# A group normalisation rewritten with hand-set semaphores: PE and VectorE in loops, VectorE taking over GpSimd's scaling and part of PE's sums

## Chip, cores, metric

One core of a Trainium2 chip. The metric is the device time of one launch in microseconds (us). Both kernels were timed several times; nearly all runs of a kernel agree within 0.3%. The record marks every run as fast or slow, by its time against the fastest run of the same kernel; all runs quoted here were fast, except that a single run (e4, e7) has no such mark.

Names: PE is the matrix engine, DVE is VectorE, ACT is ScalarE, POOL is GpSimd, SP is the engine that issues the transfers. A "DMA engine" is one of the core's 16 transfer engines. PSUM is the memory that PE writes its sums to; a chunk is 512 neighbouring elements of a partition's row.

## The reference

```python
# x: (128, 1024, 32, 16) bf16; g, b: (1024,) bf16; G = 32 groups of 32 channels
xr = x.reshape(B, G, C // G, H, W)
mu = xr.mean(axis=(2, 3, 4), keepdims=True)
var = ((xr - mu) ** 2).mean(axis=(2, 3, 4), keepdims=True)
xn = ((xr - mu) / jnp.sqrt(var + 1e-5)).reshape(B, C, H, W)
return xn * g[None, :, None, None] + b[None, :, None, None]
```

The input is 134 MB and the output is 134 MB. A tile is 4 samples by 32 groups on 128 partitions, with 32 channels of 512 elements along a partition: 4 MB (4096 KB in the profile). There are 32 tiles, numbered 0 to 31.

## The kernel before

It is written in a framework that sets the waits by itself. Six slots hold tiles. Cut to what the argument touches:

```python
XBUFS = 6; UPFRONT = 6; AHEAD = 5; QUARTERS = 4
STORE_IN_PARTS = 2; LAST_SHARE = 3; POOL_SHARE = 13
...
def L(i):                                  # load, on SP's queue
    xt = xpool.tile([P, F], BF16, name="xt")
    parts = NQ if i == 0 or i >= NT - 1 else 1
    w = F // parts
    for c in range(parts):
        ... nc.sync.dma_start(out=xt[:, c*w:(c+1)*w], in_=x_v[i][:, c*w:(c+1)*w])
...
def matmuls(st, name, lo, hi):             # PE adds the 32 chunks of a tile in PSUM
    for k in range(lo, hi):
        ... matmul(out=ps, lhsT=eye, rhs=st["xt"][:, k*MMN:(k+1)*MMN], ...)
...
def squares(st, w, k, bias, scale, sq):    # ACT, two halves per tile, sum in accum_out
...
def A(i):                                  # scale and shift: POOL 13 channels, DVE 16
    if not in_parts(i):
        for n in range(POOL_SHARE):
            scale_on("pool", i, KC - LAST_SHARE - POOL_SHARE + n)
        for k in range(KC - LAST_SHARE - POOL_SHARE):
            scale_on("dve", i, k)
    ...                                    # last two tiles: stores in quarters
def finish(i):                             # ACT takes the last 3 channels
    for k in range(KC - LAST_SHARE, KC):
        scale_on("act", i, k)
    S(i, 0, NQ)                            # one store of the tile
    j = i + AHEAD
    if UPFRONT <= j < NT:
        L(j)                               # waits until the store of tile i-1 has landed
...
for i in range(NT):
    Q(i)                                   # squares of i, with finish(i-1) in the middle
    if i + 1 < NT:
        M(i + 1); R0(i + 1)                # sums of i+1
    V(i)                                   # 1/sqrt, then scale and shift factors
    A(i)
```

## Time and profile before

| | before |
|---|---|
| time, median | 634.59 us when it was given; 634.62 us in four runs beside the changed kernel |
| profiled span | 631.9 us |
| bytes moved | 268.44 MB |
| rate, 61 to 552 us | 432 GB/s, DMA share 1.00 |
| busy ACT / DVE / POOL / PE | 85% / 60% / 55% / 46% |
| spacing of the stores in the middle | 19.4 us |

From the profile's page: the busy time of each engine; then the DMA share and the rate in 40 equal slices of the span (9 means at least 90%); then the data queue with packets, MB and share of 16 engines' span.

```profile
span 631.9 us, 3907 instructions
...
PE 293.1 (46%) x1025; PEld 114.4 (18%) x1025; DVE 380.2 (60%) x645; ACT 539.0 (85%) x268; POOL 346.8 (55%) x523
...
DMA  8999999999999999999999999999999999999996
GB/s 365 431 437 423 430 431 429 431 433 431 424 430 432 431 431 429 430 433 438 428 432 429 433 431 429 430 430 433 434 431 431 430 430 432 433 426 436 433 418 271
...
q1 hardware_dynamic: 10944, 268.44, 99.0%
```

No compute engine is above 85%, the queue is at 99%. The first slice is a ramp and the last slice a tail; between them the rate stays near 431.

The groups of instructions: count, then busy us and mean ns of one, then the idle time before them and what ended it.

```profile
L244 ACT ACTIVATE ja<-xt,negmean 128x8192 fp8e5<-128x8192 bf16 x60 | 426.7, 7112 | 52.1 <-DVE jd L189 52.0
...
L368 DVE TENSOR_SCALAR xt<-xt,scl,bia 128x512 bf16<-128x512 bf16 x536 | 352.6, 732 | 40.0 <-POOL bia L353 40.0
L368 POOL TENSOR_SCALAR xt<-xt,scl,bia 128x512 bf16<-128x512 bf16 x390 | 308.7, 806 | 3.4 <-POOL bia L353 0.3
```

ScalarE has 60 such squares of 7.1 us; the scaling of a channel is recorded as 732 ns on DVE and 806 ns on POOL.

Busy time in four stretches, from the table of windows (start and end in us, length, busy us and counts by engine, PE clock, DMA share, GB/s; other windows below have the same columns, less the engines that were idle throughout):

```profile
core 0: us, PE busy (x) PEld busy (x) DVE busy (x) ACT busy (x) POOL busy (x), PEclk, DMA share, GB/s
61.00:552.00 491.00, 231.47 (x800) 89.70 (x800) 312.24 (x499) 440.55 (x211) 299.52 (x446) 0.71 1.00 432
600.00:616.00 16.00, 0.00 (x0) 0.00 (x0) 11.04 (x37) 10.95 (x13) 0.00 (x0) 0.50 0.98 415
616.00:624.00 8.00, 0.00 (x0) 0.00 (x0) 0.00 (x0) 0.00 (x0) 0.00 (x0) 0.50 1.00 421
624.00:632.00 8.00, 0.00 (x0) 0.00 (x0) 0.00 (x0) 0.00 (x0) 0.00 (x0) 0.50 0.29 123
```

Steady transfers hold to 624 us. All arithmetic has ended by 616 us, and the last 8 us are DMA engines finishing at different times: the 16 completions of the last store come between 623.81 and 630.98 us.

SP's issues from the timeline, which show the steady rhythm (start us, us, engine, line, operation, out<-in, count; the same columns in every timeline below):

```profile
start us, us, engine line op out<-in xcount [idle before <-releaser]
...
435.47 0.34 SPq L101 DMA_DIRECT2D xt<-in_x_dram  x1
435.91 0.37 SPq L381 DMA_DIRECT2D out_dram<-xt  x1
454.84 0.34 SPq L101 DMA_DIRECT2D xt<-in_x_dram  x1
```

Each load is issued when the store that last used its slot has landed, and the next store follows at once; a pair comes every 19.4 us, which is 8.39 MB (one load and one store of 4.19 MB) at 432 GB/s. The store was ready and queued behind the waiting load.

DVE's scaling of tiles 29 and 30 from the timeline:

```profile
574.25 11.14 DVE L368 TENSOR_SCALAR xt<-xt,scl,bia 128x512 bf16<-128x512 bf16 x16 [1.29 <-POOL bia L353]
...
591.23 5.26 DVE L368 TENSOR_SCALAR xt<-xt,scl,bia 128x512 bf16<-128x512 bf16 x16 [1.29 <-POOL bia L353]
```

Sixteen channels take 11.14 us while POOL scales too, and 5.26 us when POOL rests, a factor of 2.1.

### The profile page before, as it was taken

How to read it: one execution, taken by the hardware profiler on the slowest of the kernel's cores; microseconds unless marked ns; L12 is line 12 of the kernel's file. 1: busy time of each engine (PE TensorE's matmuls, PEld its weight loads, DVE VectorE, ACT ScalarE, POOL GpSimd, SP SyncE). 2: the span in 40 equal slices, each digit the busy share in tenths (PEclk: the TensorE clock that was granted, in tenths of full speed). 3: DMA queues.
4: the chain of work that ended last, by engine and by line, in shares of the span. 5: the costliest groups of instructions: out<-in, count | busy, mean ns of one | idle time of the engine just before them, and what ended most of it. 6: DMA issues, size and time to landing. Idle time of an engine off the chain costs nothing.

```text
span 631.9 us, 3907 instructions
## 1 busy us (share of the span) xinstructions
PE 293.1 (46%) x1025; PEld 114.4 (18%) x1025; DVE 380.2 (60%) x645; ACT 539.0 (85%) x268; POOL 346.8 (55%) x523
## 2 busy tenths in 40 slices
PE   5578604553245633456433565335553345647000
PEld 2233201221112211122111222112221112213000
DVE  1087666666676576545775457754657654577660
ACT  4589999999999897877997779977989797797960
POOL 0077666666666576544775446764557654477100
PEclk9689758766787657876678766677865788658655
DMA  8999999999999999999999999999999999999996
GB/s 365 431 437 423 430 431 429 431 433 431 424 430 432 431 431 429 430 433 438 428 432 429 433 431 429 430 430 433 434 431 431 430 430 432 433 426 436 433 418 271
DMA packets 11063, 268.70 MB, mean 425 GB/s; under 512 B 1312, under 2 KB 1312, under 8 KB 1312
## 3 DMA queue, kind: packets, MB, share of 16 engines
q1 hardware_dynamic: 10944, 268.44, 99.0%
q8 instruction: 8, 0.13, 0.1%
q14 instruction: 15, 0.12, 0.0%
q10 hardware_dynamic: 96, 0.00, 0.0%
HBM read 134.22 MB, written 134.22 MB: 425 GB/s over the span
## 4 chain that ended last, share of the span: by engine, by line
DMA 67%; ACT 15%; PE 7%; issue 4%; DVE 3%; POOL 0%; SPq 0%; DVEq 0%; ACTq 0%; POOLq 0%
DMA out_dram<-xt 42%; DMA xt<-in_x_dram 25%; ACT ja L244 13%; PE pa L166 7%; DVE xt L368 3%; ACT xt L363 2%; DMA gb_b<-in_g_dram 1%; POOL scl L337 0%; SPq L101 0%; ACT rstd L308 0%; DVE rstd L312 0%; DVE jd L189 0%; POOL shift L343 0%; DVEq L455 0%; DVE bia L324 0%
## 5 line engine op out<-in xcount | busy, mean ns | idle before, releaser
L244 ACT ACTIVATE ja<-xt,negmean 128x8192 fp8e5<-128x8192 bf16 x60 | 426.7, 7112 | 52.1 <-DVE jd L189 52.0
L166 PE MATMUL pa<-xt,eye 128*128 128x512 bf16 x976 | 281.8, 460 | 289.7 <-DMA xt<-in_x_dram 278.5
L368 DVE TENSOR_SCALAR xt<-xt,scl,bia 128x512 bf16<-128x512 bf16 x536 | 352.6, 732 | 40.0 <-POOL bia L353 40.0
L368 POOL TENSOR_SCALAR xt<-xt,scl,bia 128x512 bf16<-128x512 bf16 x390 | 308.7, 806 | 3.4 <-POOL bia L353 0.3
L166 PEld LDWEIGHTS <-eye 128*128 128x128 bf16 x1024 | 114.3, 114 | 468.5 <-DMA xt<-in_x_dram 290.6
L337 POOL TENSOR_SCALAR scl<-gb,rstd 128x32 f32<-128x32 f32 x31 | 11.2, 361 | 218.2 <-DVE rstd L312 218.2
L189 DVE TENSOR_SCALAR_CACHE_REDUCE jd<-pa 128x512 bf16<-128x512 f32 x32 | 22.0, 688 | 149.0 <-PE pa L166 149.0
L363 ACT ACTIVATE xt<-xt,bia,scl 128x512 bf16<-128x512 bf16 x98 | 72.0, 798 | 0.8 <-DVE bia L324 0.8
L244 ACT ACTIVATE ja<-xt,q 128x4096 fp8e5<-128x4096 bf16 x8 | 29.6, 3706 | 6.6 <-DVE jd L189 6.4
L312 DVE RECIPROCAL rstd<-rstd 128x1 f32<-128x1 f32 x32 | 5.1, 160 | 35.8 <-ACT rstd L308 35.8
L343 POOL TENSOR_SCALAR shift<-scl,negmean 128x32 f32<-128x32 f32 x31 | 11.2, 360 | 3.1
L216 POOL TENSOR_SCALAR off<-negmean,q 128x1 f32<-128x1 f32 x2 | 0.9, 432 | 20.5 <-DVE jd L189 20.5
L166 PE MATMUL pb<-xt,eye 128*128 128x512 bf16 x48 | 11.6, 388 | 1.0 <-DMA xt<-in_x_dram 1.0
L308 ACT ACTIVATE rstd<-s,v 128x1 f32<-128x1 f32 x30 | 8.8, 294 | 2.8
L244 ACT ACTIVATION_READ_ACCUMULATOR ja<-xt,negmean 128x1 f32 x60 | 11.2, 187 | 0.0
L353 POOL TENSOR_TENSOR bia<-shift,gb 128x32 f32<-128x32 f32 x31 | 7.8, 252 | 2.6
L308 ACT ACTIVATE rstd<-var,eps_t 128x1 f32<-128x1 f32 x2 | 0.6, 295 | 9.2 <-DVE jv L292 9.2
L273 POOL TENSOR_SCALAR v<-s 128x1 f32<-128x1 f32 x30 | 5.8, 192 | 2.5
L156 DVE COPY gb<-gb_p 128x64 f32<-128x64 f32 x1 | 0.2, 224 | 5.6 <-PE gb_p L148 5.6
L116 ACT ACT_TABLE_LOAD x1 | 1.3, 1283 | 1.7 <-PEq L444 1.7
L189 DVE DVE_READ_ACCUMULATOR jd<-pa 128x1 f32 x32 | 2.6, 81 | 0.0
L292 DVE TENSOR_SCALAR_CACHE_REDUCE jv<-sq,seed 128x4 f32<-128x4 f32 x2 | 0.4, 216 | 2.7 <-ACT ja L244 2.7
(18 smaller groups left out, 6.1 us busy)
## 6 DMA issues: line engine op xcount, KB each, us to landing
xt<-in_x_dram SPq DMA_DIRECT2D x30, 4096.0 KB, 29.3
out_dram<-xt SPq DMA_DIRECT2D x30, 4096.0 KB, 38.3
xt<-in_x_dram SPq DMA_DIRECT2D x8, 1024.0 KB, 16.5
out_dram<-xt SPq DMA_DIRECT2D x8, 1024.0 KB, 17.8
gb_b<-in_g_dram ACTq DMA_DIRECT2D x1, 2.0 KB, 3.2
gb_b<-in_b_dram ACTq DMA_DIRECT2D x1, 2.0 KB, 5.3
```

The source lines that it names most:

```text
L116: chain("act", nc.scalar.activation(out=warm[:], in_=eps_t[:], func=ACT.Sqrt))
L166: nc.tensor.matmul(out=ps[:], lhsT=eye[:], rhs=st["xt"][:, k * MMN : (k + 1) * MMN], start=(k == lo), stop=(k == hi - 1),),
L189: nc.vector.tensor_scalar(out=jd[:], in0=ps[:], scalar1=-inv_n, scalar2=seed, op0=ALU.mult, op1=ALU.add, accum_out=total[:],),
L244: nc.scalar.activation(out=ja[:, 0:w], in_=st["xt"][:, k * w : (k + 1) * w], func=ACT.Square, bias=bias, scale=scale, accum_out=sq, satura ...
L273: nc.gpsimd.tensor_scalar(out=v0[:], in0=s0[:], scalar1=inv_n, scalar2=EPS, op0=ALU.mult, op1=ALU.add,),
L308: nc.scalar.activation(out=rstd[:], in_=last_sum[:], func=ACT.Sqrt, bias=bias[:], scale=scale),
L312: chain("dve", nc.vector.reciprocal(out=rstd[:], in_=rstd[:]))
L337: nc.gpsimd.tensor_scalar(out=scl[:], in0=gam, scalar1=rstd[:], scalar2=None, op0=ALU.mult),
L343: nc.gpsimd.tensor_scalar(out=shift[:], in0=scl[:], scalar1=st["negmean"][:], scalar2=None, op0=ALU.mult,),
L353: nc.gpsimd.tensor_tensor(out=bia[:], in0=shift[:], in1=bet, op=ALU.add),
L363: inst = nc.scalar.activation(out=span, in_=span, func=ACT.Identity, bias=bia, scale=scl)
L368: inst = eng.tensor_scalar(out=span, in0=span, scalar1=scl, scalar2=bia, op0=ALU.mult, op1=ALU.add,)
```

## The change

The intent: take the framework's waits and the sharing between DVE and POOL out of the way, and balance the work. Each engine gets its own program; PE and DVE loop over six tiles a trip. POOL scales nothing, DVE scales 29 channels; PE adds 20 chunks and DVE the other 12, as pairs. The scale and shift factors move from POOL to DVE, which summed the means before too. The core of the diff:

```diff
-XBUFS = 6
-UPFRONT = 6
+SLOTS = 6
+FIRST = 2
 AHEAD = 5
-STORE_IN_PARTS = 2
-ACT_SHARE = 2
-LAST_SHARE = 3
-POOL_SHARE = 13
+PE_CHUNKS = 20
+ACT_SHARE = 3
+LAST_ACT_SHARE = 4
...
+    loaded = per_slot("loaded")        # 14 semaphores for each of 6 slots, and 5 more
+    stored = per_slot("stored")
...
+    ctx.callback(lambda: nc.clear_and_free_semaphores(sems))
+    block = ctx.enter_context(nc.Block())
+    @block.sync
+    def _(sp):
...
+        for i in range(SLOTS):
+            load(i)                    # each in one piece
+        for i in range(NT):
+            n = nth(i)
+            if i < NT - 1:
+                store(i, 0, KC, n, n)
+            else:
+                store(i, 0, KC // 2, n, n)
+                store(i, KC // 2, KC, n + 1, n + 1)
+            j = i + AHEAD
+            if SLOTS <= j < NT:
+                load(j)
...
+    @block.tensor
+        with loop(pe):                 # 20 matmuls a tile, six tiles a trip
+            for i in range(FIRST, FIRST + SLOTS):
+                add_chunks(*in_loop(i, regs["w1"], regs["w2"]))
...
+    @block.vector
+        def mean(s, count, count16):
+            inst = dve.scalar_tensor_tensor(   # 3072 pairs, the other 12 chunks
+                out=jd[:],
+                in0=xts[s][:, PE_CHUNKS * MMN : PE_CHUNKS * MMN + PAIRS],
+                scalar=1.0,
+                in1=xts[s][:, PE_CHUNKS * MMN + PAIRS : F],
+                op0=ALU.mult, op1=ALU.add, accum_out=col(s, HALF), ...
+        with loop(dve):
+            for i in range(FIRST, FIRST + SLOTS):
+                ...
+                mean(s, c, w)
+                ...
+                factors(s, c)
+                apply(s, 0, KC - ACT_SHARE, c)
...
+    @block.scalar                      # ACT: as before, but no early root, and all tiles in halves
+        for i in range(NT):
+            squares(i, 0)
+            if i:
+                apply(i - 1, KC - ACT_SHARE, KC)
+            squares(i, 1)
+            root(i)
```

## The prediction

> **What bounds the kernel now.** The transfers. The page shows 268.44 MB on the one data queue, busy for 99.0% of 16 engines' span, mean 425 GB/s. The table of windows gives 432 GB/s from 61 to 552 us at a DMA share of 1.00. Compute has room: ACT 85%, DVE 60%, POOL 55%, PE 46%. [...] At 432 the bytes alone take 621 us. The rest of the 631.9 us span is the ramp (full rate from about 3 us) and the tail, where the engines run dry one by one from 624 to 631 us (windows of 1 us).
>
> **What the change does.**
> - Same 268 MB, same order of loads and stores, six slots, same load-ahead. The loads of the first and last tile go from four pieces to one, the store of tile 30 from four to one, of tile 31 from four to two.
> - POOL stops scaling (309 us of busy time). DVE scales 29 channels instead of 16. Where POOL is idle (591 to 596 us, timeline) 16 took 5.26 us, 0.33 us each; beside POOL 16 took 11.14 us. Estimate for 29: 9.5 us, less than now. DVE also adds 12 chunks as 3072 pairs: from the 0.69 us of the 512-element reduction, an estimate of 3.3 to 4.1 us. In all some 15 us of DVE per tile.
> - PE adds 20 chunks instead of 32: about 6 us instead of 9.
> - ACT keeps two squares of 7.1 us, three channels (2.1 us), accumulator reads and root: about 16.8 us per tile.
> - Fewer instructions to fetch; all fetches are 0.25 MB now, estimate 0.5 us.
>
> The period per tile is 19.4 us (spacing of the stores in the timeline), set by DMA. The longest engine, ACT, stays at 16.8, so nothing removed is on the critical path.
>
> **Start.** Tile 0 lands whole near 13 us; squares begin near 21 us instead of 9.6. But before, tile 0's factors waited for tile 1's sum (33.5 us) anyway. I expect store 0 near 46 us, as before (46.8), then one every 17 us. Loads keep the queue full to about 61 us, so no gap opens.
>
> **End.** The last load lands near 582; estimate: sum at 589, squares to 606, stores issued about 600 (tile 30), 611 and 615 (before: 614.6). The queue still holds about 15 us of work then, so the tail stays DMA's.
>
> **Prediction.** 634 us, 8 in 10 between 629 and 639. Chances: faster by over 2%: 0.02; within 2%: 0.94; slower by over 2%: 0.04.
>
> **What would show it right.** DMA rows at 9 throughout with about 430 GB/s; DVE busy between 380 and 500 us; its scaling instruction down from 732 ns to about 400 as recorded; POOL nearly idle; ACT about 530 us busy; stores paced at 19.4 us after about tile 8. A wrong step would show as a slice below 420 GB/s: near 60 to 80 us if the first stores come late, at the end if the last halves come after the queue drained.
>
> **What would make it wrong.** The pair addition several times slower than estimated, or ACT and DVE waiting for each other, so that a tile takes over 19.4 us; stalls at the loops' back branches[...]; a square-root table reloaded per tile; a DMA rate that changes when POOL's accesses vanish; barriers and semaphore clearing at the end costing over 2 us.

Two passages are cut from the recorded text. 621 us for the bytes at 432 GB/s and some 11 us of ramp and tail make the span of 631.9 us, the device time of that kernel was 634.59 us, and the forecast of 634 leaves it as it is.

## The result, and the profile after

The changed kernel took 635.11 us in the median of four runs (633.96 to 635.80), against 634.62 us (633.94 to 634.77) for the kernel before. The ratio is 1.0008, 95% interval 0.9991 to 1.0025: the same. A ratio here and below is the mean time of one kernel's fast runs over that of the other's of the same rounds, so it is not quite the ratio of the medians quoted.

The same parts of the page after:

```profile
span 633.0 us, 3032 instructions
...
PE 207.1 (33%) x641; PEld 75.7 (12%) x641; DVE 456.7 (72%) x1181; ACT 540.5 (85%) x263; POOL 12.8 (2%) x38
...
DMA  8999999999999999999999999999999999999994
GB/s 365 430 433 413 437 433 431 431 429 431 429 431 439 431 435 433 433 435 433 433 431 431 431 429 433 437 433 435 433 435 433 433 431 433 431 431 433 435 427 195
...
q1 hardware_dynamic: 9360, 268.44, 98.6%
```

PE's and POOL's busy time fell by 86 and 334 us, DVE's rose by 77 us, and the rows of the transfers hardly moved. The queue's share is 98.6%. The fourth slice shows 413 GB/s (423 before); it is where the first stores begin, and over the first 61 us both kernels moved 412 GB/s.

The groups after:

```profile
L375 ACT ACTIVATE ja<-xt,sm 128x8192 fp8e5<-128x8192 bf16 x64 | 455.2, 7112 | 68.0 <-DVE sm L294 67.9
...
L331 DVE TENSOR_SCALAR xt<-xt,scl,bia 128x512 bf16<-128x512 bf16 x923 | 301.2, 405 | 1.2
L269 DVE SCALAR_TENSOR_TENSOR jd<-xt 128x3072 fp8e5<-128x3072 bf16 x32 | 107.3, 3354 | 46.0 <-DMA xt<-in_x_dram 43.6
...
L393 ACT ACT_TABLE_LOAD x1 | 1.3, 1283 | 0.0
```

ACT still has its 7.1 us squares, now 64. The last line is a second table load on ACT, 1283 ns, once, at the first root (L393): it starts at 35.84 us, right after the read of the accumulator, and the root starts at 37.13 us. The other load (1283 ns, L375) stands before the first square. The kernel before, whose first function is a root, has one load only (1283 ns, L116).

The four stretches after:

```profile
61.00:552.00 491.00, 164.03 (x500) 59.70 (x500) 380.98 (x983) 445.32 (x217) 10.30 (x27) 0.68 1.00 432
600.00:616.00 16.00, 0.00 (x0) 0.00 (x0) 8.50 (x27) 11.35 (x11) 0.00 (x0) 0.50 1.00 432
616.00:624.00 8.00, 0.00 (x0) 0.00 (x0) 0.00 (x0) 0.00 (x0) 0.00 (x0) 0.50 0.91 389
624.00:633.00 9.00, 0.00 (x0) 0.00 (x0) 0.00 (x0) 0.00 (x0) 0.00 (x0) 0.50 0.11 49
```

The middle is again 432 GB/s. In the tail the DMA share falls from 0.91 before 624 us to 0.11 after, and the last of the last store's 16 completions comes 7.4 us behind the first. SP's issues after:

```profile
436.52 0.34 SPq L166 DMA_DIRECT2D xt<-in_x_dram  x1
436.95 0.44 SPq L177 DMA_DIRECT2D out_dram<-xt  x1
455.88 0.34 SPq L166 DMA_DIRECT2D xt<-in_x_dram  x1
```

The pairs of load and store are again 19.4 us apart. DVE's scaling of tile 29 after:

```profile
571.29 9.47 DVE L331 TENSOR_SCALAR xt<-xt,scl,bia 128x512 bf16<-128x512 bf16 x29
```

It has 29 channels in 9.47 us, less than the 16 took beside POOL.

Two ends, read from the trace's records of completions and of semaphore instructions (us from the start of the span):

```
                          last completion of a transfer   end of the span   between
before                    630.98                          631.95            0.97
after                     630.96                          633.01            2.06
```

In these two profiled executions the transfers ended at the same time. The changed kernel then spent 1.1 us more: it clears its 89 semaphores in one POOL instruction of 526 ns (the one clear at the end of the kernel before took 96 ns) and passes two more barriers.

### The profile page after: what moved, and what is told of

It reads as the page before. It is cut to its first block, busy times and chain, and to the rows that moved or that the text cites. A ratio compares the mean times of both kernels' runs of the same rounds, so it can differ in the third digit from the quotient of the medians.

```text
span 633.0 us, 3032 instructions
## 1 busy us (share of the span) xinstructions
PE 207.1 (33%) x641; PEld 75.7 (12%) x641; DVE 456.7 (72%) x1181; ACT 540.5 (85%) x263; POOL 12.8 (2%) x38
## 3 DMA queue, kind: packets, MB, share of 16 engines
q1 hardware_dynamic: 9360, 268.44, 98.6%
## 4 chain that ended last, share of the span: by engine, by line
DMA 67%; ACT 20%; DVE 5%; issue 3%; PE 2%; SPq 1%; DVEq 0%
DMA out_dram<-xt 61%; ACT ja L375 17%; DMA xt<-in_x_dram 7%; DVE xt L331 4%; ACT xt L407 2%; PE ps L237 2%; SPq L166 0%; ACT sm L393 0%; DVE jd L282 0%; ACT L393 0%; DVE bia L317 0%; DVE scl L308 0%; DVE sm L305 0%; DVE sm L294 0%; DVEq _compat.py:109 0%
## 5 line engine op out<-in xcount | busy, mean ns | idle before, releaser
L375 ACT ACTIVATE ja<-xt,sm 128x8192 fp8e5<-128x8192 bf16 x64 | 455.2, 7112 | 68.0 <-DVE sm L294 67.9
L237 PE MATMUL ps<-xt,eye 128*128 128x512 bf16 x640 | 206.9, 498 | 370.9 <-DMA xt<-in_x_dram 370.9
L331 DVE TENSOR_SCALAR xt<-xt,scl,bia 128x512 bf16<-128x512 bf16 x923 | 301.2, 405 | 1.2
L269 DVE SCALAR_TENSOR_TENSOR jd<-xt 128x3072 fp8e5<-128x3072 bf16 x32 | 107.3, 3354 | 46.0 <-DMA xt<-in_x_dram 43.6
L237 PEld LDWEIGHTS ps<-xt,eye 128*128 128x128 bf16 x640 | 75.6, 123 | 501.8 <-DMA xt<-in_x_dram 386.3
L282 DVE TENSOR_SCALAR_CACHE_REDUCE jd<-ps,sm 128x512 fp8e5<-128x512 f32 x32 | 24.0, 751 | 69.4 <-PE ps L237 69.0
L222 POOL TENSOR_SCALAR sm<-sm 128x1 f32<-128x1 f32 x32 | 12.0, 376 | 582.6 <-ACT ja L375 582.6
L375 ACT ACTIVATION_READ_ACCUMULATOR ja<-xt,sm 128x1 f32 x64 | 12.0, 187 | 0.0
L393 ACT ACTIVATE sm<-sm 128x1 f32<-128x1 f32 x32 | 9.4, 295 | 1.0
L317 DVE SCALAR_TENSOR_TENSOR bia<-scl,sm,gb 128x32 f32<-128x32 f32 x32 | 8.0, 251 | 1.1
L375 ACT ACT_TABLE_LOAD x1 | 1.3, 1283 | 1.9 <-issue 1.9
L393 ACT ACT_TABLE_LOAD x1 | 1.3, 1283 | 0.0
```

Of the source, the lines that this page charges most:

```text
L222: inst = pool.tensor_scalar(out=col(s, VAR), in0=col(s, SQ), scalar1=inv_n, scalar2=EPS, op0=ALU.mult, op1=ALU.add,)
L237: inst = pe.matmul(out=banks[s][:], lhsT=eye[:], rhs=xts[s][:, k * MMN : (k + 1) * MMN], start=(k == 0), stop=(k == PE_CHUNKS - 1),)
L269: inst = dve.scalar_tensor_tensor(out=jd[:], in0=xts[s][:, PE_CHUNKS * MMN : PE_CHUNKS * MMN + PAIRS], scalar=1.0, in1=xts[s][:, PE_CHUNKS ...
L282: inst = dve.tensor_scalar(out=jd[:, 0:MMN], in0=banks[s][:], scalar1=1.0, scalar2=col(s, HALF), op0=ALU.mult, op1=ALU.add, accum_out=col( ...
L317: inst = dve.scalar_tensor_tensor(out=bia[s][:], in0=scl[s][:], scalar=col(s, NEG), in1=bet, op0=ALU.mult, op1=ALU.add,)
L331: inst = dve.tensor_scalar(out=span, in0=span, scalar1=scl[s][:, k : k + 1], scalar2=bia[s][:, k : k + 1], op0=ALU.mult, op1=ALU.add,)
```

## Experiments

The theory: the transfers alone set the time, and ACT, the busiest compute engine, has about 2.7 us of slack per tile. The rivals: (a) the arithmetic still holds the transfers back, and a gain of the rewrite was given back elsewhere; (b) a part of the change was worth time on its own. Runs made together share the runs of the kernel before on the same chip.

| run | median us | ratio to before (95%) |
|---|---|---|
| e1 copy only | 633.59 | 0.9989 (0.9973 to 1.0006) |
| e2 before, POOL scales nothing | 636.45 | 1.0040 (1.0023 to 1.0056) |
| e3 after, 6 channels on ACT | 639.53 | 1.0089 (1.0072 to 1.0106) |
| e4 after, 9 channels on ACT | 706.09 | one run |
| e5 after, about half the bytes | 574.35 | 0.9052 (0.9037 to 0.9067) |
| e6 before, about half the bytes | 567.93 | 0.8959 (0.8944 to 0.8974) |
| e7 copy with probes | 633.94 | one run |
| e8 after, stores of 8 neighbouring rows | 643.58 | 1.0138 (1.0121 to 1.0154) |
| e9 after, stores of 16 rows | 637.55 | 1.0043 (1.0030 to 1.0057) |
| e10 before, stores of 8 neighbouring rows | 642.13 | 1.0122 (1.0106 to 1.0137) |
| e11 before, loads and a store in one piece | 634.42 | 0.9999 (0.9985 to 1.0013) |
| e12 after, stores of 8 rows four apart | 638.40 | 1.0062 (1.0049 to 1.0076) |

The kernel before took 634.06 us (median) beside e1 to e4, 634.11 beside e5 to e7, 634.48 beside e8 to e11 and 634.64 beside e12.

### e1: the transfers without any arithmetic

```diff
-            sp.wait_ge(done_v[s], count_v)
...
-            inst._wait_ge(done_a[s], count_a)
+            inst._wait_ge(loaded[s], 16 * nth(i))
...
-    # the programs of POOL, PE, DVE and ACT
```

> The changed kernel's transfers in the same order, with no compute at all; each store waits only for its own load (wrong output on purpose). Theory (transfers alone set the time): within 1% of both kernels, about 631 us, because 268.44 MB at the 432 GB/s of the steady stretch take 621 us and the ramp and the tail some 10. Rival (the arithmetic still holds the transfers back somewhere, and the rewrite's gain was given back there): clearly faster, 622 us or less.

Measured: 633.59 us, ratio 0.9989 to the kernel before. Window of the middle (here of engines only POOL, then the clock, the DMA share and GB/s):

```profile
61.00:552.00 491.00, 0.00 (x0) 1.00 1.00 432
```

With the compute engines idle, the middle moves the same 432 GB/s. So neither kernel's arithmetic adds more than some 0.4% to its transfers. Rival (a) is out: no version of the arithmetic can gain even 1% while the transfers stay as they are. The expected 631 us was 2.6 us too low, because the estimate was a profiled span (it was 631.7 here) and the device time is some 2 us longer.

### e2: only the end of the sharing with POOL, on the kernel before

```diff
-POOL_SHARE = 13
+POOL_SHARE = 0
```

> One part of the change alone on the kernel before: GpSimd scales nothing, VectorE scales 29 channels. Theory: GpSimd busy falls from 347 us to under 45, the VectorE scaling from 732 ns to about 400 as recorded, and the time stays within 1% of before. Rival (the end of the sharing with GpSimd is worth time by itself and another part of the change lost it again): faster by over 1%.

Measured: 636.45 us, 1.0040 (1.0023 to 1.0056).

```profile
L368 DVE TENSOR_SCALAR xt<-xt,scl,bia 128x512 bf16<-128x512 bf16 x926 | 302.3, 415 | 39.8 <-POOL bia L353 39.8
```

DVE's scaling fell from 732 to 415 ns as recorded, as expected, and POOL's busy time to 58 us (expected: under 45; its remaining small work took longer, the second term of the variance 832 ns instead of 192). The time stayed within 1% but went up, not down. The last transfer completed at 633.6 us instead of 631.0, while the mean completion of the 16 last ones was 627.5 in both. So the last completion came 2.6 us later at the same mean; why this edit makes it later is not settled. The gain that rival (b) asks for is not there. The split of the sums between PE and DVE and the hand-set waits were not run alone; e1 bounds what all of them could be worth.

### e3 and e4: how much slack ACT has

```diff
-ACT_SHARE = 3
+ACT_SHARE = 6     # e4: 9
```

> The changed kernel with 6 channels a tile on ScalarE instead of 3 (VectorE 26). From the trace of the changed kernel, ScalarE takes 16.66 us per tile when nothing holds it, and 0.70 us per channel, so 18.8 us per tile, still under the 19.4 us that the transfers take. Theory: within 1% of the changed kernel, 635 us, with less idle time on ScalarE. Rival (ScalarE's chain is on the critical path, as the chain of waits shows it up to 154 us): 2.1 us per tile, some 67 us longer.

> The changed kernel with 9 channels a tile on ScalarE (VectorE 23): 20.9 us per tile, now over the 19.4 us of the transfers. Theory: ScalarE becomes the limit, stores come 20.9 us apart, and the time is about 700 us (first square at 21 us, 32 tiles at 20.9, then the last scaling and store); the DMA share falls under 95%. Rival (there is far more slack than the spacing says): near 635 us.

Measured: e3 639.53 us, e4 706.09 us. In e4 the stores come 20.9 us apart:

```profile
553.09 0.34 SPq L177 DMA_DIRECT2D out_dram<-xt  x1
...
573.99 0.33 SPq L177 DMA_DIRECT2D out_dram<-xt  x1
...
594.90 0.33 SPq L177 DMA_DIRECT2D out_dram<-xt  x1
```

That is the expected 20.9 us per tile, and the total missed by 6 us of 706. The queue's share on the page is 92.1%. So the slack lies between 2.1 us per tile (e3, which still moves 432 GB/s from 61 to 552 us) and 4.2 us, as the spacing of 19.4 against 16.7 us said. Rival (a) would have had e3 near 700 us.

e3 was not free: 0.8% above the changed kernel by the two ratios, where within 1% was expected. Its windows at the end show the reason (columns as in the windows of the kernel before):

```profile
561.00:600.00 39.00, 13.80 (x39) 5.00 (x40) 26.67 (x68) 38.90 (x25) 5.76 (x2) 0.68 1.00 430
600.00:624.00 24.00, 0.00 (x0) 0.00 (x0) 14.08 (x46) 23.17 (x19) 0.35 (x1) 0.50 0.61 264
624.00:640.00 16.00, 0.00 (x0) 0.00 (x0) 3.58 (x12) 1.48 (x3) 0.00 (x0) 0.52 0.62 262
```

The rate falls to 264 GB/s already from 600 us on. With almost no slack per tile the arithmetic no longer runs ahead, so the last two tiles are computed after the queue has emptied; all 16 last completions come at 634.8 to 634.9 us. The end is where spent slack shows first.

### e5 and e6: both kernels with about half the bytes

In both, from tile 6 on only the first half of a tile is loaded and, for all tiles but the last, only half is stored; the bytes fall from 268.44 to 148.90 MB. The outputs are wrong.

```diff
 # e5, in the changed kernel
+                if i >= SLOTS:
+                    w = HF
...
-                store(i, 0, KC, n, n)
+                store(i, 0, KC // 2, n, n)
 # e6, in the kernel before
-        w = F // parts
+        w = F // parts if i < UPFRONT else F // 2
+        # and the last tile's half is loaded in one piece
...
-        S(i, 0, NQ)
+        S(i, 0, NQ // 2)
+    # reads of the second half go to the first half (sums, squares)
+    # or to a constant chunk (scaling)
```

> The changed kernel with all its arithmetic, but from tile 6 on only half of each tile is loaded, and of all tiles but the last only half is stored (wrong output on purpose; the other half of a slot is old data). The transfers then need about 10 us per tile, so what is left is the arithmetic. Theory: ScalarE sets the pace at 16.7 us per tile and the time is about 570 us (21 + 1.3 + 31 x 16.7 + 15 + 10 + 7). If the transfers were not the limit before, about 635.

> The same for the kernel before: half of each tile loaded from tile 6 on and half stored of all but the last; the arithmetic is of the same count and shapes (the second half of the sums and squares reads the first half again, the second half of the scaling reads one constant chunk; wrong output on purpose). Theory: ScalarE has the same work in both kernels, so about 570 us here too, within 2% of the other half-byte run: the change gains nothing even where the transfers do not hide it. Rival (the change freed time that only the transfers hide): this one is longer than the other by over 2%[...].

Measured: 574.35 and 567.93 us. Both are now set by ACT, which is busy for over 99% of the time from 61 to 500 us in both: stores come 16.7 us apart (first e5, then e6; the last line of each merges all later stores).

```profile
482.35 0.33 SPq L179 DMA_DIRECT2D out_dram<-xt  x1
...
499.01 65.36 SPq L179 DMA_DIRECT2D out_dram<-xt  x6
```

```profile
480.71 0.33 SPq L393 DMA_DIRECT2D out_dram<-xt  x1
...
497.42 62.43 SPq L393 DMA_DIRECT2D out_dram<-xt  x9
```

So even with the transfers out of the way the change gains nothing per tile: it shortened DVE's, POOL's and PE's work, and ACT has the same squares in both. The e6 run is even 1.1% faster, which I did not expect. The timelines show where: the last tile's root on ACT (one line each), first e5 and then e6.

```profile
555.03 0.30 ACT L395 ACTIVATE sm<-sm 128x1 f32<-128x1 f32 x1
```

```profile
550.52 0.29 ACT L319 ACTIVATE rstd<-var,eps_t 128x1 f32<-128x1 f32 x1 [0.39 <-DVE jv L303]
```

The root comes 4.5 us later in the changed kernel (555.03 against 550.52 us). Nearly all of that is there already at the start: tile 1's first square starts at 37.9 us instead of 33.3, because tile 0 is summed only when all of it has landed (its first square starts at 21.9 us in e5, and at 10.1 in e6), and the table load of 1.28 us sits in that chain. The longer end adds 1.1 us; the last store, of twice the size, probably the rest, which was not taken apart. The late start exists in the real kernels too; there the full queue hides it (e11).

### e7: which DMA engines come last

The copy of e1, with 15 tiny loads over 1, 2, ... 15 partitions queued behind all stores:

```diff
+        for k in range(1, 16):
+            sp.dma_start(
+                out=probe[0:k, 256 * k : 256 * (k + 1)], in_=x_v[0][0:k, 0:256]
+            ).then_inc(probed[k - 1], 16)
```

> The copy with 15 tiny loads queued at the end, over 1, 2, ... 15 partitions, each with its own semaphore, to see which DMA engines are the last to run dry (wrong output on purpose). In the changed kernel's trace 12 of the 16 completions of the last store come within 1.1 us and the other four up to 7.4 us later. Theory (a few given engines are slower the whole time): the same spread[...]. Rival (the spread comes from the order of the last stores): the spread is gone or random here. The time is about 1 us over the copy's.

The completions of some probes, from the trace's records of semaphores (us from the start; the issuing engine's own count at issue is left out):

```
 8 partitions: 623.96 624.29 624.39 624.57 624.95 625.08 625.13 625.46
 9 partitions: 624.16 624.49 624.60 624.75 625.12 625.25 625.33 625.65 628.50
11 partitions: 624.32 624.58 624.89 625.01 625.11 625.47 625.61 625.68 625.80 626.03 628.84
12 partitions: 624.50 624.79 625.10 625.22 625.31 625.65 625.79 625.87 625.97 626.22 629.02 629.14
14 partitions: 624.24 624.29 624.85 625.21 625.52 625.63 625.67 626.00 626.14 626.23 626.32 626.61 629.36 629.50
15 partitions: 624.40 624.45 625.02 625.42 625.72 625.85 625.86 626.18 626.31 626.41 626.49 626.79 627.73 629.54 629.67
```

A load over n partitions left n completions (8 for 8, 15 for 15). The steps from 8 to 9 partitions, from 11 to 12 and from 14 to 15 each add a late one: in the largest probe they lie 0.9, 2.8 and 2.9 us behind the last of the others. None of the 8 completions over 8 partitions is late. Four completions are late in e1 and in the changed kernel; the fourth is in no probe. The records give no engine's number, so which engines are late was not shown. That the late completions belong to the same few engines in every transfer, and that a store over 8 partitions leaves these engines out, was my assumption; e8 is built on it. The run took 633.94 us, 0.35 us over the copy where about 1 us was expected.

The lateness builds up, but not evenly: in e1 the first and the last completion of one transfer lie 0.5 us apart at 72 us, still 0.9 at 169, then 3.0 at 249 and 5.4 at 387 us, and from 440 us on they stay 5.9 to 6.2 us apart up to the last whole tile. So the late completions do not come from engines that are slower by a fixed share the whole time, as the expectation had it; why they fall behind, and why they then stop falling behind, was not tested. The last of 16 sets the end. This answers what the tail is made of: in e1 twelve of the 16 have completed by 624.8 us and the last at 629.7.

### e8 and e9: shifting work off the late engines

In the changed kernel, 12 channels of tile 30's store are cut by rows: in e8 into 16 stores of 8 neighbouring partitions, which by my assumption leave the late engines out; in e9, the control, into 8 stores of 16, which by the same assumption use all of them.

```diff
+            if i == NT - 2:
+                store(i, 0, KC - TURNED, n, n)            # TURNED = 12
+                for r in range(0, P, ROWS):               # ROWS = 8; e9: 16
+                    sp.dma_start(
+                        out=o_v[i][r : r + ROWS, (KC - TURNED) * HW : F],
+                        in_=xts[slot(i)][r : r + ROWS, (KC - TURNED) * HW : F],
+                    ).then_inc(stored[slot(i)], 16)
```

> The changed kernel with 12 of 32 channels of the store of tile 30 cut into 16 stores of 8 partitions each[...]. 3/8 of a tile is 3.6 us of one engine. Theory (the slowest engines set the end): the last completions come near 627.5 instead of 631.0[...], and the time falls by about 3.5 us, 0.5%. Rival[...]: no gain or a loss.

> Control for the former: the same channels in 8 stores of 16 partitions each[...]. Theory: the same spread of the last completions as in the changed kernel, and the same time within 0.2% (about 635 us). Rival (the gain comes from smaller stores, not from the choice of engines): as fast as with 8 partitions.

The 3.6 us of e8 are an estimate: 12 of 32 channels of a tile of 4.19 MB at the 432 GB/s of the trace.

Measured: 643.58 and 637.55 us. Both lose against the kernel before, e8 1.4%, where a gain of 0.5% on the changed kernel was expected. The windows of e8 at the end (columns as in the windows of the changed kernel):

```profile
600.00:610.00 10.00, 0.00 (x0) 0.00 (x0) 4.21 (x14) 9.17 (x9) 0.00 (x0) 0.50 0.98 422
610.00:615.00 5.00, 0.00 (x0) 0.00 (x0) 4.29 (x14) 2.21 (x4) 0.00 (x0) 0.50 0.67 188
615.00:625.00 10.00, 0.00 (x0) 0.00 (x0) 0.00 (x0) 0.00 (x0) 0.00 (x0) 0.50 0.40 112
```

The rate falls to 188 and 112 GB/s while these stores run. SP's issues of them:

```profile
599.44 22.84 SPq L192 DMA_DIRECT2D out_dram<-xt  x16
622.37 3.53 SPq L179 DMA_DIRECT2D out_dram<-xt  x2
```

SP needed 22.8 us to issue the 16 small stores (0.8 to 1.0 us each for the first nine, up to 3.1 us later; a whole tile takes it 0.33 us), so the last tile's two stores, ready at about 610 and 614 us, could be issued only from 622.4 us. Single packets of these stores (12 KB) took up to 4226 ns; the median was 460. How much of the 22.8 us is issuing and how much is waiting for slow packets was not separated. Whether it matters that the 8 rows are neighbours, e12 tests. The control was wrong too: it was expected within 0.2% of the changed kernel and lost about 0.35%, so row-wise small stores cost something over 16 rows too. It is not a clean control, because its 16 rows are neighbours too, and its longest 12 KB packet took 3415 ns, nearly as long as in e8.

### e10: the same on the kernel before

The edit is that of e8 with tile 30's last two quarters stored as 4 channels in one piece and 12 channels in 16 stores of 8 partitions.

> The same on the kernel before: tile 30's last 12 channels, 4 in one store and 12 in 16 stores of 8 partitions, in place of two quarters of 8 channels. Theory: the time falls by some 2 to 3.5 us against the kernel before, to about 631 us, less than on the changed kernel because its engines end more evenly. It is also about 1 us faster than the changed kernel with the same stores, because its end costs 1.0 us after the last completion and not 2.1.

Measured: 642.13 us, a loss of 1.2%, against an expected gain of 2 to 3.5 us. The path of the loss is not quite that of e8: here each issue took SP only 0.3 to 0.9 us, but the framework's waits held the fifth small store back from 603.9 to 612.0 us, until an earlier store had landed, and the last tile's stores went out from 625.3 us.

### e11: the pieces alone

```diff
-        parts = NQ if i == 0 or i >= NT - 1 else 1
+        parts = 1
...
-STORE_IN_PARTS = 2
+STORE_IN_PARTS = 1
```

> One part of the change alone on the kernel before: every load in one piece, and the store of tile 30 in one piece; tile 31's store stays in four. Theory (the early sums of tile 0 and the small last pieces buy nothing while the queue is full): the first square starts near 23 us or later instead of 9.6, and the time stays within 0.3% of before, 633 to 636 us. Rival: the late start or end adds 2 us or more.

Measured: 634.42 us, ratio 0.9999 (0.9985 to 1.0013). The first square started at 17.4 us instead of 9.6 (expected: 23 or later, an error of mine: this kernel still makes its first sum from the first quarter of the tile). A start 8 us later costs nothing, because the first six loads (25.2 MB, 58 us at 432 GB/s, from about 3 us on) fill the queue to about 61 us in any case.

### e12: 8 rows four apart

```diff
-                for r in range(0, P, ROWS):
+                for r in (0, 64, 32, 96, 1, 65, 33, 97, 2, 66, 34, 98, 3, 67, 35, 99):
...
-                        out=o_v[i][r : r + ROWS, (KC - TURNED) * HW : F],
-                        in_=xts[slot(i)][r : r + ROWS, (KC - TURNED) * HW : F],
+                        out=o_v[i][r : r + 29 : 4, (KC - TURNED) * HW : F],
+                        in_=xts[slot(i)][r : r + 29 : 4, (KC - TURNED) * HW : F],
```

> As the run with 16 stores of 8 neighbouring partitions, but each store takes 8 partitions four apart (0, 4, ... 28 and so on). [...] Theory[...]: the loss is gone, the last completions come near 627.5, and the time falls to about 632 us, 0.5% below the changed kernel. Rival 1 (small stores by themselves cost the loss): again about 640 us. Rival 2[...]: near 635 us or a little over, no gain.

My causes for the theory and for rival 2, which no run shows, are cut; what is left is the question whether 8 rows four apart lose less than 8 neighbours.

Measured: 638.40 us, 1.0062 (1.0049 to 1.0076). The longest packet of these stores fell from 4226 to 898 ns, and 5 of the 8 to 9 us of e8's loss are gone. So the way the rows are dealt to the stores was a real part of that loss. By what it acts was not shown: the rows lie four times as far apart in the output too, and the order of the stores changed; neither was tested apart. The windows from 610 us and SP's issues:

```profile
610.00:615.00 5.00, 0.00 (x0) 0.00 (x0) 3.66 (x12) 1.57 (x3) 0.00 (x0) 0.50 0.63 238
615.00:625.00 10.00, 0.00 (x0) 0.00 (x0) 0.00 (x0) 0.00 (x0) 0.00 (x0) 0.50 0.91 368
```

```profile
598.82 17.11 SPq L192 DMA_DIRECT2D out_dram<-xt  x16
616.03 2.30 SPq L179 DMA_DIRECT2D out_dram<-xt  x2
```

SP still needed 17.1 us for 16 small stores, so the last tile's stores went out from 616.0 us (in the changed kernel the last was issued at 614.4), and the rate dipped to 238 GB/s in between. The test whether work can be shifted off the late engines is therefore spoiled: the queue ran low while SP was held up. Besides, e7 ran on another chip than e8 to e12, and that the same completions are late there was not probed. Why they are late stays open. No version faster than the two kernels was found.

## Why the prediction was right

- **"The transfers" bound the kernel.** Right. The copy without arithmetic takes as long (e1, 0.9989), and with about half the bytes both kernels fall to some 570 us, where ACT's pace of 16.7 us per tile sets the time (e5, e6).
- **"Nothing removed is on the critical path."** Right. DVE, PE and POOL were relieved and ACT was not. ACT's slack was stated as 19.4 minus 16.8 us per tile; e3 (2.1 us more, +0.8%) and e4 (4.2 us more, 706 us) lie on the two sides of it.
- **DVE's costs.** Right: 29 channels in 9.46 us (estimate 9.5), the pair addition 3.35 us (estimate 3.3 to 4.1: six times 0.69 us is 4.1, and it is 3.3 if 0.16 us of the 0.69, the DVE's reciprocal of one element on the page, is paid once), DVE busy 457 us (380 to 500), scaling recorded as 405 ns (about 400). These are readings of the changed kernel's trace.
- **The start.** Right: the squares begin at 21.4 us (about 21), the first store is issued at 47.8 (about 46), and no gap opens. e11 shows on the kernel before that a first square 8 us later costs nothing.
- **The end.** Right: stores issued at 599.0 and, the last, at 614.4 us (600 and 615), with some 16 us of transfers still to come; the last completion is at 630.96 us, before it was at 630.98.
- **What was small or missed.** The barriers and the clearing of semaphores cost 1.1 us more, under the 2 us named as a risk. The square-root table was not reloaded per tile but once, 1.28 us, hidden by the full queue. The instruction fetches fell from 0.25 to 0.08 MB. ACT was busy for 540.5 us, where about 530 was expected. One slice between the ramp and the tail fell below 420 GB/s (413, the fourth), which the prediction named as a sign of a wrong step; the first 61 us still moved 412 GB/s in both kernels, so it cost nothing. The loops' back branches left no gap in the rhythm: the pairs of load and store stay 19.4 us apart through all trips. Why PE's and DVE's relief does not even show with the transfers out of the way, because ACT had the same work, was implied by "the longest engine, ACT, stays at 16.8" and is shown by e5 and e6.

## What to carry to other kernels

When one queue is full from start to end at its steady rate, first time the transfers alone; that number bounds every rewrite of the arithmetic (here 633.59 us against 634.06, e1). Read the slack of the busiest compute engine from the spacing of the stores against its own work per tile, and do not spend all of it, because the last tiles then come after the queue has emptied (264 GB/s from 600 us on, e3). A rewrite that takes load off engines other than the busiest one can be worth nothing even where nothing hides it (stores 16.7 us apart in both, e5 and e6).
